# Where the next batch is scaled, turned and tidied in a state-space and feed-forward kernel

## The chip, the cores and the metric

The kernel runs on one core of one Trainium2 chip. Its time is the device time of one execution in microseconds (us); a kernel's time is the median over several executions. The engines of the core are PE (TensorE, the matrix unit, with its weight loads listed as PEld), DVE (VectorE), ACT (ScalarE), POOL (GpSimd) and SP (SyncE, here only a queue that issues transfers). Each engine takes its instructions in the order in which they stand, and waits on semaphores for the others.

## The reference

Two layers follow each other. The first is a chunked state-space layer, for 4 batches, 8 heads, 768 tokens, head size 32 and state size 16, in chunks of 32 tokens; the second is a gated feed-forward layer from 256 to 1536 and back to 256 columns.

```python
log_a = np.log(np.clip(a, 1e-06, 1.0))
state = np.zeros((batch, H, N, D), dtype=np.float32)
for c in range(nc):
    ...                                             # xc, Bc, Cc, la: this chunk
    cum = np.cumsum(la, axis=-1)
    L = np.exp(cum[:, :, :, None] - cum[:, :, None, :]) * causal
    CB = np.einsum('bhin,bhjn->bhij', Cc, Bc)
    y_intra = np.einsum('bhij,bhjd->bhid', CB * L, xc)
    y_inter = np.einsum('bhin,bhnd->bhid', Cc, state) * np.exp(cum)[:, :, :, None]
    y[:, :, sl] = y_intra + y_inter
    ...
    state = decay_full[:, :, None, None] * state + np.sum(Bx, axis=2)
x = y.transpose(0, 2, 1, 3).reshape(B * S, H * D)   # 3072 tokens x 256
out = (np.maximum(x @ w_gate, 0.0) * (x @ w_val)) @ w_out
```

Since the decay between two tokens is a product of the a between them, it can be split into a factor of the one token and the inverse factor of the other. The kernel does that: C is scaled by a running product FC, B by its reciprocal FB, and no chunk has to be treated alone.

## The kernel before

**Tiling.** The 3072 tokens are cut into 12 pairs of 128-token chunks, three pairs to a batch (`PPB`), and into 6 blocks of 512 tokens, two pairs to a block. The loop at line 442 runs over the blocks. Block b does the feed-forward layer of its 512 tokens, and in between, the state-space layer of later pairs: in the loop P = 2b+2, Q = 2b+3 and W = 2b+1.

**Preparing a batch.** Rows of B and C are loaded with `load_rows` (line 75), 384 KB each. `factors` (160) makes FC from the running product of a, with two scans and two transposes on DVE; `inverse` (179) makes FB by a reciprocal. `scale` (193) multiplies half of B or C by its factor, giving sqB and sqC: two calls for each of B and C. `turn` (202) transposes a whole sq tile on DVE into tqB or tqC. `tidy_b` (208) and `tidy_c` (220) copy a range of tq's rows, in token order, into BT and CT, where matmuls read them; CT has two halves, t = 0 and 1, masked by tmask. Eleven rows are 264 tokens, so rows 0 to 11, 11 to 22 and 22 to 32 cover the three pairs of a batch.

**A pair.** `cast_x` (231) makes bf16 xb out of the loaded xr. `rows_b` (242) transposes B back by PE (tile bb) and copies it (bt). `G` (252) multiplies B and C into four banks g; `gevac` (270) empties these with ACT (lines 277, 280) and DVE (283, 285), with POOL's causal mask (266). `astep` (290) adds a chunk to the state in the bank A_ps, and `sevac` (299) copies it, masked, to Sm on DVE; `state` (305) is both. `inter` (314) and `Dm` (326) form y from Sm and from gs, and `yevac` (340) writes yT by ACT.

**A block.** The first four of the twelve column groups f are done in two halves of 256 tokens (`gvh`, 366: tiles gv and r, product h), the others whole (`gv`, 352: tiles gate, val, r and h, ACT at 363, DVE at 364). `fout` (382) multiplies h with w_out four times, twelve matmuls each (line 387), and `foevac` (392) copies the result and stores it from SP. At the head of each block SP also issues the rows of the next batch and two pairs of x (lines 445 to 450). SP is a queue in order: these loads stand behind the preceding block's last store.

**Order.** Nothing is scheduled: `in_order` (16) fixes each engine's instructions as the Python code issues them. `prep` (456) places the preparation of batch b+1 in block b: its steps 0 and 1 at f = 4 and 5 (reciprocal, then the scales of B and C on POOL), steps 2 and 3 at f = 6 and 7 (turn B, turn C), and steps 4 to 6 at f = 8 to 10 (tidy a third of the rows of B and of C's first half on ACT, of C's second half on POOL). `at` (452) gives f for the other insertions, for blocks 0, 1, and 2 on.

**Banks.** Of the PSUM banks six are shared (`bank`, 69) by w, bb, g, gv, gate, val and o. A matmul that takes one waits for the engine that emptied it before.

**The start.** The first part of a and B go out on SP's queue, C on ACT's (lines 92 to 95). `keep_warm` (129) runs matmuls without use. The first weights are loaded by POOL (`weights`, 140) after B has landed, which `wait_for` (153) sees to.

Of the kernel before, what the change touches and what calls it, by code (L numbers as in the profile page):

```python
# [30 lines left out]
def kernel(  # L31
# [13 lines left out]
    nc = tc.nc  # L45

    NB, NH, S, D = x.shape
# [5 lines left out]
    NPAIR = T // 256  # L53
    PPB = NC // 2
    NBLK = T // 512
    R = 32
# [32 lines left out]

    al = const.tile([128, 2 * NB, K + 1], FP32)  # L90
    av = a.rearrange("b (t q) (r k) -> (q r) (b t) k", t=2, r=R)
    nc.sync.dma_start(out=al[:, 0:2, 1:], in_=av[:, 0:2])
    rows = {}
    rows["C", 0] = load_rows(C, 0, nc.scalar, "cr")
    rows["B", 0] = load_rows(B, 0, nc.sync, "br")
# [33 lines left out]
    def keep_warm(n):  # L129
        w = bank("w")  # L130
        for _ in range(n):
            nc.tensor.matmul(out=w, lhsT=warm[:, 0:128], rhs=warm, start=True, stop=True)

    keep_warm(13)

    wg = glob.tile([128, 2, DF], BF16)
    wv = glob.tile([128, 2, DF], BF16)
# [8 lines left out]
    def weights_out(f0, f1):  # L146
        nc.gpsimd.dma_start(
            out=wo[:, f0:f1, :],
            in_=moe_w_out[f0 * 128:f1 * 128, :].rearrange("(o i) m -> i o m", i=128))
# [3 lines left out]
    def wait_for(j, cell):  # L153
        nc.gpsimd.tensor_copy(gate[:, j:j + 1], cell)
# [24 lines left out]
    def inverse(b):  # L179
        nc.vector.reciprocal(FB[:, 2 * b:2 * b + 2], FC[:, 2 * b:2 * b + 2])  # L180
# [12 lines left out]
    def scale(j, b, t, eng):  # L193
        if (j, b) not in sq:
            sq[j, b] = glob.tile([128, KK, 2 * N, 2], BF16, name="sq%s%d" % (j, b))
        f = (FB if j == "B" else FC)[:, 2 * b + t].rearrange("p (a k) -> p a k", k=2)
        eng.tensor_tensor(  # L197
            out=sq[j, b][:, :, t * N:(t + 1) * N, :],
            in0=rows[j, b][:, t].rearrange("p (a k n) -> p a n k", n=N, k=2),
            in1=f.unsqueeze(2).to_broadcast([128, KK, N, 2]), op=ALU.mult)  # L200

    def turn(j, b):
        tq[j, b] = glob.tile([128, KK, R, 2], BF16, name="tq%s%d" % (j, b))
        nc.vector.transpose(  # L204
            tq[j, b].rearrange("p a r k -> p (a r k)").bitcast(U32),
            sq[j, b].rearrange("p a n k -> p (a n k)").bitcast(U32))

    def tidy_b(b, r0, r1, eng):
        dst = BT[b][:, K * r0:K * r1]
        src = tq["B", b][:, :, r0:r1, :]  # L210
        if eng is nc.scalar:
            eng.copy(out=dst.rearrange("p (r a k) -> p r a k", a=KK, k=2),
                     in_=src.rearrange("p a r k -> p r a k"))
        else:
            eng.tensor_copy(
                dst.bitcast(U32).rearrange("p (r a) -> p r a", a=KK),
                tq["B", b].rearrange("p a r k -> p (a r k)").bitcast(U32)
                .rearrange("p (a r) -> p r a", r=R)[:, r0:r1])

    def tidy_c(b, t, r0, r1, eng):  # L220
        dst = CT[b][:, t, K * r0:K * r1].rearrange("p (r a k) -> p r a k", a=KK, k=2)
        src = tq["C", b][:, :, r0:r1, :].rearrange("p a r k -> p r a k")
        if eng is nc.scalar:
            eng.mul(dst, src, tmask[:, t:t + 1])  # L224
        else:
            eng.tensor_scalar_mul(dst, src, tmask[:, t:t + 1])

    yT = glob.tile([128, 2, T], BF16)
    A_ps = mm.tile([128, 2, 128], FP32, tag="Aps", name="A_ps")
# [40 lines left out]
    def gevac(p, half=True):  # L270


        s = st[p]
        g = [t.rearrange("j i t m -> j (i t) m") for t in s["gp"]]
        d = s["gs"]
        m = maskUT.to_broadcast([128, 4, 128])
        nc.scalar.copy(out=d[:, 0], in_=g[0])  # L277
        causal(d[:, 0], 4)
        h = 2 if half else 0
        nc.scalar.copy(out=d[:, 1, h:4], in_=g[1][:, h:4])  # L280
        causal(d[:, 1, h:4], 4 - h)
        for q in (2, 3):
            nc.vector.tensor_tensor(out=d[:, q], in0=g[q], in1=m, op=ALU.mult)  # L283
        if half:
            nc.vector.tensor_tensor(out=d[:, 1, 0:2], in0=g[1][:, 0:2], in1=m[:, 0:2],
                                    op=ALU.mult)
# [18 lines left out]
    def state(p, i):  # L305
        astep(p, i)
        sevac(p, i)
# [58 lines left out]
    def gvh(b, f, u):  # L366

        if f == 0 and u == 0:
            fst[b] = ffn.tile([128, NF, 512], BF16, tag="h", name="h")
        tk = slice(b * 512 + u * 256, b * 512 + (u + 1) * 256)  # L370
        fs = slice(f * 128, (f + 1) * 128)
        gv_ = bank("gv", (128, 2, 256))
        for j, w in ((0, wg), (1, wv)):
            for k in range(2):
                nc.tensor.matmul(out=gv_[:, j], lhsT=w[:, k, fs], rhs=yT[:, k, tk],  # L375
                                 start=(k == 0), stop=(k == 1), skip_group_check=True)
        r = ffn.tile([128, 512], BF16, tag="r", name="r", bufs=3)[:, 0:256]
        nc.scalar.activation(r, gv_[:, 0], AF.Relu)  # L378
        nc.vector.tensor_tensor(out=fst[b][:, f, u * 256:(u + 1) * 256], in0=r,  # L379
                                in1=gv_[:, 1], op=ALU.mult)  # L380
# [42 lines left out]
    G(0)  # L423
    astep(0, 0)
    gevac(0, half=False)
    tidy_b(0, 11, R, nc.vector)
    sevac(0, 0)
    tidy_c(0, 0, 11, R, nc.scalar)
    tidy_c(0, 1, 11, R, nc.vector)
    wait_for(1, st[1]["xr"][0:1, 1, 0, 0:1])  # L430
    weights(4, 8)
    load_x(2, nc.sync, after=nc.gpsimd)
    keep_warm(4)
    Dm(0)
    inter(0, 1)
    astep(0, 1)
# [5 lines left out]
    for b in range(NBLK):  # L442
        P, Q, W = 2 * b + 2, 2 * b + 3, 2 * b + 1
        more = P < NPAIR
        if b < 3:
            for j, src in (("B", B), ("C", C)):
                rows[j, b + 1] = load_rows(src, b + 1, nc.sync, j.lower() + "r")
        for n in (P + 1, P + 2):
            if n < NPAIR:
                load_x(n, nc.sync)  # L450

        def at(name, *fs):

            return more and f == fs[min(b, len(fs) - 1)]

        def prep(step):
            n = b + 1
            if n >= NB:
                return
            if step == 0:  # L460
                inverse(n)
            if step < 2:
                scale("B", n, step, nc.gpsimd)
                scale("C", n, step, nc.gpsimd)
            elif step < 4:
                turn("BC"[step - 2], n)
            elif step < 7:
                r = 11 * (step - 4)
                r1 = min(r + 11, R)
                tidy_b(n, r, r1, nc.scalar)  # L470
                tidy_c(n, 0, r, r1, nc.scalar)
                tidy_c(n, 1, r, r1, nc.gpsimd)

        for f in range(4):
            gvh(b, f, 0)
            if b == 0 and f == 0:
                gevac(1)
            if b == 0 and f == 1:
                cast_x(1, nc.scalar)
                state(1, 0)  # L480
                weights(8, NF)
                wait_for(2, st[2]["xr"][0:1, 1, 0, 0:1])
                weights_out(0, NF)
            if f == (3 if b == 0 else 1):
                if b == 1:
                    state(W, 1)
                inter(W, 0)
                inter(W, 1)
                Dm(W)
                if b == 0:  # L490
                    state(1, 1)
                yevac(W, nc.scalar)
        for f in range(4):
            gvh(b, f, 1)
        for f in range(4, NF):
            if b == 0 and f == 4:
                factors(2, 8)
            gv(b, f)
            if f in (4, 5):
                prep(f - 4)  # L500
            if f >= 6:
                prep(f - 4)
            if at("cast P", 6, 4, 4):
                cast_x(P, nc.gpsimd)
            if at("cast Q", 8, 5, 4):
                cast_x(Q, nc.gpsimd)
            if at("rows P", 7, 6, 5):
                rows_b(P)
            if at("state P0", 9, 8, 7):
                state(P, 0)  # L510
            if at("state P1", 10, 10, 9):
                state(P, 1)
            if at("rows Q", 99, 9, 8):
                rows_b(Q)
        if more:
            inter(P, 0)
            inter(P, 1)
        fout(b, 0)
        foevac(b, 0)
        if more:  # L520
            G(P)
            gevac(P)
        if b == 0:
            rows_b(Q)
        fout(b, 1)
        foevac(b, 1)
        if more and b > 0:
            state(Q, 0)
        fout(b, 2)
        foevac(b, 2)  # L530
        if more:
            Dm(P)
            yevac(P, nc.scalar)
            G(Q)
            gevac(Q)
            state(Q, 1 if b else 0)
        fout(b, 3)
        foevac(b, 3)

# [31 lines left out]
```

## Time and profile before

| what | us |
|---|---|
| median of 6 runs (range) | 138.75 (138.35 to 139.23) |
| the profiled execution | 138.35 |
| its span | 136.2 |
| PE busy | 118.9 (87%) |
| DVE busy | 91.4 (67%) |
| ACT busy | 83.2 (61%) |
| POOL busy | 43.5 (32%) |
| PE clock granted | full, in all 40 slices |

The span goes from the first to the last recorded instruction; an execution takes 2.15 us more than that here. A share of busy time is an average over unlike stages, so the blocks are looked at one by one: block 0 begins at 12.76 us, blocks 1 to 5 at 37.24, 58.34, 80.39, 98.62 and 116.75. Batches 1, 2 and 3 are prepared in blocks 0, 1 and 2. In a line of the timeline the first number is the start, the second the duration; the bracket at the end gives the idle time of the engine just before and the instruction that ended it. "gs<-g" means that gs is written and g read; where several instructions are put together, xN stands behind the shapes.

### The profile page before, as it was taken

Reading aid. Unit: us, or ns where it says so; the run is one execution under the profiler, and the core shown is the slowest. Engines: PE = TensorE matmul, PEld = TensorE weight load, DVE = VectorE, ACT = ScalarE, POOL = GpSimd, SP = SyncE. Lnnn points to the kernel's source line nnn. Section 1 sums busy time; section 2 is a strip of 40 time slices with the busy share of each in tenths; the row PEclk is TensorE's granted clock in tenths of the full one; section 3 lists DMA queues with packets and bytes.
Section 4 is the critical chain, followed back from the end, with each engine's and each line's share of the span. In section 5 each row is a group of like instructions: output and inputs, shape, how many; then the busy total and the mean of one; then the engine's idle time right before and its main releaser. Section 6 shows DMA issues by size and latency. Waiting matters only on the chain.

```text
span 136.2 us, 2883 instructions
## 1 busy us (share of the span) xinstructions
PE 118.9 (87%) x1057; PEld 76.5 (56%) x1057; DVE 91.4 (67%) x204; ACT 83.2 (61%) x181; POOL 43.5 (32%) x74
## 2 busy tenths in 40 slices
PE   6957588488999967999767999999999999999990
PEld 2324463156785435786324778457785467864680
DVE  6974969576479477569377567786577865697611
ACT  4274676294587485588467478773598645886510
POOL 3435631975111981220974240102221002200000
PEclk9999999999999999999999999999999999999999
DMA  4995999950259500239800024700251002200022
GB/s 117 242 163 89 192 226 251 213 84 0 84 130 274 58 0 5 77 93 273 102 1 0 0 82 116 118 0 2 82 127 27 0 5 77 77 5 0 0 77 77
DMA packets 34686, 12.07 MB, mean 89 GB/s; under 512 B 26481, under 2 KB 34673, under 8 KB 34673
## 3 DMA queue, kind: packets, MB, share of 16 engines
q1 hardware_dynamic: 30928, 8.88, 30.4%
q0 software_dynamic: 3184, 2.36, 12.1%
q10 hardware_dynamic: 560, 0.66, 1.5%
q8 instruction: 8, 0.13, 0.4%
q14 instruction: 6, 0.04, 0.1%
HBM read 11.11 MB, written 3.15 MB: 105 GB/s over the span
## 4 chain that ended last, share of the span: by engine, by line
PE 53%; DMA 13%; ACT 8%; POOL 8%; DVE 8%; issue 6%; SPq 0%; DVEq 0%; POOLq 0%; ACTq 0%
PE o L387 20%; PE gv L375 9%; DMA br<-in_B_dram 8%; PE val L360 8%; PE gate L357 8%; DMA wv<-in_moe_w_val_dram 5%; POOL sqB L197 3%; DVE h L364 3%; PE g L259 2%; ACT r L363 2%; POOL sqC L197 2%; PE y L332 2%; ACT CT L224 2%; POOL xb L234 2%; ACT r L378 1%
## 5 line engine op out<-in xcount | busy, mean ns | idle before, releaser
L364 DVE TENSOR_TENSOR h<-r,val 128x512 bf16<-128x512 bf16 x48 | 32.5, 679 | 8.5 <-ACT r L363 8.2
L387 PE MATMUL o<-wo,h 128*128 128x256 bf16 x288 | 35.1, 273 | 2.3 <-DVE h L364 2.3
L363 ACT ACTIVATE r<-gate 128x512 bf16<-128x512 f32 x48 | 28.6, 596 | 9.8 <-PE gate L357 8.6
L387 PEld LDWEIGHTS <-h 128*128 128x128 bf16 x288 | 27.4, 98 | 7.5 <-DVE h L364 3.0
L360 PE MATMUL val<-yT,wv 128*128 128x512 bf16 x96 | 28.6, 379 | 0.9 <-DMA wv<-in_moe_w_val_dram 0.4
L357 PE MATMUL gate<-yT,wg 128*128 128x512 bf16 x96 | 28.5, 379 | 0.0
L379 DVE TENSOR_TENSOR h<-r,gv 128x256 bf16<-128x256 bf16 x48 | 20.0, 421 | 8.8 <-ACT r L378 8.3
L266 POOL TENSOR_SCALAR_AFFINE_SELECT gs<-gs 128x512 bf16<-128x512 bf16 (+1 forms) x24 | 12.1, 529 | 39.9 <-ACT gs L277 39.9
L283 DVE TENSOR_TENSOR gs<-g,maskUT 128x512 bf16<-128x512 f32 x24 | 15.5, 685 | 13.4 <-PE g L259 10.3
L378 ACT ACTIVATE r<-gv 128x256 bf16<-128x256 f32 x48 | 18.5, 385 | 4.1 <-PE gv L375 2.5
L375 PE MATMUL gv<-yT,wg 128*128 128x256 bf16 x96 | 18.4, 273 | 0.5 <-ACT yT L345 0.5
L375 PE MATMUL gv<-yT,wv 128*128 128x256 bf16 x96 | 18.3, 273 | 0.5 <-DMA wv<-in_moe_w_val_dram 0.5
L357 PEld LDWEIGHTS <-wg 128*128 128x128 bf16 x96 | 9.0, 98 | 13.5 <-issue 6.5
L360 PEld LDWEIGHTS <-wv 128*128 128x128 bf16 x96 | 9.3, 98 | 12.6 <-DMA wv<-in_moe_w_val_dram 0.9
L277 ACT CAST gs<-g 128x512 bf16<-128x512 f32 x12 | 7.0, 587 | 8.0 <-PE g L259 7.9
L345 ACT CAST yT<-y 128x512 bf16<-128x512 f32 x12 | 7.0, 585 | 7.8 <-PE y L332 6.8
L295 PE MATMUL A_ps<-xb,bt 128*128 128x256 bf16 x20 | 5.5, 274 | 6.8 <-POOL xb L234 2.9
L375 PEld LDWEIGHTS <-wg 128*128 128x128 bf16 x96 | 9.0, 98 | 4.0 <-issue 2.6
L375 PEld LDWEIGHTS <-wv 128*128 128x128 bf16 x96 | 9.3, 98 | 1.8 <-DMA wv<-in_moe_w_val_dram 0.8
L197 POOL TENSOR_TENSOR sqB<-br,FB 128x384 bf16<-128x384 f32 x6 | 5.3, 882 | 15.7 <-DVE FB L180 15.7
L224 ACT ACTIVATE CT<-tqC,tmask 128x264 bf16<-128x264 bf16 (+2 forms) x12 | 6.4, 540 | 5.2 <-DVE tqC L204 5.2
L234 POOL CAST xb<-xr 128x512 bf16<-128x512 f32 x10 | 6.1, 612 | 10.6 <-DMA xr<-in_x_dram 10.6
(65 smaller groups left out, 108.9 us busy)
## 6 DMA issues: line engine op xcount, KB each, us to landing
xr<-in_x_dram SPq DMA_DIRECT2D x24, 128.0 KB, 4.9
out_dram<-ob SPq DMA_DIRECT2D x10, 256.0 KB, 2.2
br<-in_B_dram SPq DMA_DIRECT2D x4, 384.0 KB, 4.0
cr<-in_C_dram SPq DMA_DIRECT2D x3, 384.0 KB, 4.7
wg<-in_moe_w_gate_dram POOLq DMA_DIRECT2D x3, 256.0 KB, 4.5
wv<-in_moe_w_val_dram POOLq DMA_DIRECT2D x3, 256.0 KB, 6.4
wo<-in_moe_w_out_dram POOLq DMA_DIRECT2D x1, 768.0 KB, 10.2
cr<-in_C_dram ACTq DMA_DIRECT2D x1, 384.0 KB, 3.2
```

What stands on the lines that cost most here:

```text
L197: eng.tensor_tensor(out=sq[j, b][:, :, t * N:(t + 1) * N, :], in0=rows[j, b][:, t].rearrange("p (a k n) -> p a n k", n=N, k=2), in1=f.unsq ...
L224: eng.mul(dst, src, tmask[:, t:t + 1])
L266: nc.gpsimd.affine_select(out=dst, in_=dst, pattern=[[0, n], [1, 128]], compare_op=ALU.is_ge, fill=0.0, base=0, channel_multiplier=-1)
L283: nc.vector.tensor_tensor(out=d[:, q], in0=g[q], in1=m, op=ALU.mult)
L357: nc.tensor.matmul(out=g, lhsT=wg[:, k, fs], rhs=yT[:, k, tk], start=(k == 0), stop=(k == 1))
L360: nc.tensor.matmul(out=v, lhsT=wv[:, k, fs], rhs=yT[:, k, tk], start=(k == 0), stop=(k == 1))
L363: nc.scalar.activation(r, g, AF.Relu)
L364: nc.vector.tensor_tensor(out=fst[b][:, f], in0=r, in1=v, op=ALU.mult)
L375: nc.tensor.matmul(out=gv_[:, j], lhsT=w[:, k, fs], rhs=yT[:, k, tk], start=(k == 0), stop=(k == 1), skip_group_check=True)
L378: nc.scalar.activation(r, gv_[:, 0], AF.Relu)
L379: nc.vector.tensor_tensor(out=fst[b][:, f, u * 256:(u + 1) * 256], in0=r, in1=gv_[:, 1], op=ALU.mult)
L387: nc.tensor.matmul(out=o[:, ts % 2], lhsT=fst[b][:, f, ts * 128:(ts + 1) * 128], rhs=wo[:, f], start=(f == 0), stop=(f == NF - 1), skip_gr ...
```

## The change

The first part of a is split over SP's queue and ACT's, ahead of B and of C. In the prologue only pair 1's rows are tidied, after the first state copy; the warm-up matmuls go from 13 and 4 to 14 and 3. A function `tidy(p, ...)` does one pair's rows. It stands after the first whole f of block 0 for pair 2, after its last f for pair 3, at f = 5 of later blocks for pair Q, and near the end of each block for pair P+2, on the engines given. In block 0, pair 1's first state step moves from f = 1 to f = 3, FB is made directly after the factors, and the scales follow at f = 4 to 7, C first. In later blocks the four scales are issued at f = 0 to 3 of the first quarter, and FB is made in the block before. The turns come at f = 9 and 10 of block 0, at 8 and 10 of block 1, and in block 2 after the evacuation of G(P). The cast of P's x moves from f = 6 to 5 in block 0.

```diff
-    nc.sync.dma_start(out=al[:, 0:2, 1:], in_=av[:, 0:2])
+    nc.sync.dma_start(out=al[:, 0:1, 1:], in_=av[:, 0:1])
+    nc.scalar.dma_start(out=al[:, 1:2, 1:], in_=av[:, 1:2])
...
-    keep_warm(13)
+    keep_warm(14)
...
+    def tidy(p, b_eng, c0_eng, c1_eng):
+        b, k = p // PPB, p % PPB
+        r = slice(11 * k, min(11 * k + 11, R))
+        tidy_b(b, r.start, r.stop, b_eng)
+        tidy_c(b, 0, r.start, r.stop, c0_eng)
+        tidy_c(b, 1, r.start, r.stop, c1_eng)
...
-    tidy_b(0, 11, R, nc.vector)
     sevac(0, 0)
-    tidy_c(0, 0, 11, R, nc.scalar)
-    tidy_c(0, 1, 11, R, nc.vector)
+    tidy(1, nc.vector, nc.scalar, nc.vector)
...
-    keep_warm(4)
+    keep_warm(3)
...
-        def prep(step):
-            n = b + 1
-            if n >= NB:
-                return
-            if step == 0:
-                inverse(n)
-            if step < 2:
-                scale("B", n, step, nc.gpsimd)
-                scale("C", n, step, nc.gpsimd)
-            elif step < 4:
-                turn("BC"[step - 2], n)
-            elif step < 7:
-                r = 11 * (step - 4)
-                r1 = min(r + 11, R)
-                tidy_b(n, r, r1, nc.scalar)
-                tidy_c(n, 0, r, r1, nc.scalar)
-                tidy_c(n, 1, r, r1, nc.gpsimd)
+        new = b + 1
+
+        def scale_new(k):
+            if new < NB:
+                scale("CB"[k % 2], new, k // 2, nc.gpsimd)
+
+        def turn_new(j):
+            if new < NB:
+                turn(j, new)
 
         for f in range(4):
             gvh(b, f, 0)
             if b == 0 and f == 0:
                 gevac(1)
+            if b > 0:
+                scale_new(f)
             if b == 0 and f == 1:
                 cast_x(1, nc.scalar)
-                state(1, 0)
                 weights(8, NF)
                 wait_for(2, st[2]["xr"][0:1, 1, 0, 0:1])
                 weights_out(0, NF)
+            if b == 0 and f == 3:
+                state(1, 0)
...
         for f in range(4):
             gvh(b, f, 1)
+        if b == 0:
+            factors(2, 8)
+            inverse(1)
         for f in range(4, NF):
+            gv(b, f)
             if b == 0 and f == 4:
-                factors(2, 8)
-            gv(b, f)
-            if f in (4, 5):
-                prep(f - 4)
-            if f >= 6:
-                prep(f - 4)
-            if at("cast P", 6, 4, 4):
+                tidy(P, nc.vector, nc.scalar, nc.gpsimd)
+            if b == 0 and f < 8:
+                scale_new(f - 4)
+            if at("cast P", 5, 4, 4):
                 cast_x(P, nc.gpsimd)
             if at("cast Q", 8, 5, 4):
                 cast_x(Q, nc.gpsimd)
+            if b == 0 and f == 9 or b == 1 and f == 8:
+                turn_new("C")
+            if b == 0 and f == 10 or b == 1 and f == 10:
+                turn_new("B")
+            if b == 0 and f == 11:
+                tidy(Q, nc.vector, nc.scalar, nc.gpsimd)
+            if b > 0 and more and f == 5:
+                tidy(Q, nc.scalar, nc.scalar, nc.gpsimd)
...
         if b == 0:
             rows_b(Q)
+            inverse(2)
+        if b == 1:
+            inverse(3)
+        if b == 2:
+            turn_new("C")
+            turn_new("B")
         fout(b, 1)
...
             state(Q, 1 if b else 0)
+        if P + 2 < NPAIR:
+            tidy(P + 2, nc.vector, nc.scalar, nc.gpsimd)
         fout(b, 3)
```

## The prediction

> **What bounds the kernel now.** I read the busy table by block first, cutting the span where each block's first gate matmul starts (columns: stretch and its length, then busy time of PE, PE weight load, DVE, ACT, POOL, each with its count, then clock and DMA). These are blocks 0, 1, 2 and 3:
>
> ```profile
> 12.76:37.24 24.48, 19.16 (x173) 12.23 (x174) 16.58 (x37) 14.96 (x34) 12.22 (x18) 1.00 0.89 151
> 37.24:58.34 21.10, 18.89 (x176) 12.38 (x173) 14.68 (x31) 14.17 (x32) 9.34 (x14) 1.00 0.40 88
> 58.34:80.39 22.05, 18.94 (x178) 12.59 (x176) 14.40 (x30) 14.29 (x32) 9.54 (x15) 1.00 0.38 84
> 80.39:98.62 18.23, 18.23 (x177) 12.41 (x175) 12.96 (x26) 12.13 (x26) 3.16 (x7) 1.00 0.28 60
> ```
>
> Blocks 3 and 4 are pure TensorE: 18.23 us busy in 18.23. Blocks 0 to 2, which also prepare the next batch's B and C, take 6.25, 2.87 and 3.82 us more. Only these 13 us can be won. The list of waits, kept to PE, says on what they go:
>
> ```profile
> PE A_ps L295 <- POOL xb L234: 2.9, 2, 1.9
> PE o L387 <- DVE h L364: 2.3, 3, 0.9
> PE A_ps L295 <- DVE Sm L303: 2.1, 2, 1.3
> ```
>
> PE waits for the cast of x behind POOL's scales, and for products h and states Sm that stand in DVE's queue behind the two transposes ("turn"), which wait for the scales themselves. Block 2 in the timeline (start, duration, engine, line, idle before and its releaser):
>
> ```profile
> 64.89 0.89 POOL L197 TENSOR_TENSOR sqB<-br,FB 128x384 bf16<-128x384 f32 x1 [5.95 <-DVE FB L180]
> ...
> 66.56 1.17 POOL L234 CAST xb<-xr 128x512 bf16<-128x512 f32 x2
> 67.22 0.27 PE L295 MATMUL A_ps<-xb,bt 128*128 128x256 bf16 x1 [1.00 <-POOL xb L234]
> ...
> 68.61 0.58 DVE L204 STREAM_TRANSPOSE tqB<-sqB 128x384 uint32<-128x384 uint32 x1 [2.32 <-POOL sqB L197]
> ...
> 70.61 0.27 PE L295 MATMUL A_ps<-xb,bt 128*128 128x256 bf16 x1 [1.28 <-DVE Sm L303]
> ...
> 74.75 0.28 PE L387 MATMUL o<-wo,h 128*128 128x256 bf16 x1 [0.84 <-DVE h L364]
> ```
>
> So POOL was free 5.95 us before its first scale and started it when FB came, at 64.8. But C for that batch was issued at 60.10 and took 4.7 us to land, also 64.8: an earlier scale is held by the load.
>
> **1. The split load of a.**
>
> ```profile
> 0.80 0.43 SPq L92 DMA_DIRECT2D al<-in_a_dram  x1
> 0.80 0.49 ACTq L77 DMA_DIRECT2D cr<-in_C_dram  x1
> ...
> 2.74 0.08 DVE L183 MEMSET zero<- 128x31 f32 x1
> 2.78 0.26 DVE L161 TENSOR_TENSOR_SCAN prod<-al,one 128x50 f32<-128x50 f32 x1
> ```
>
> The scan at 2.78 follows DVE's memsets without a gap, so an earlier a gains nothing. C is now issued behind a half of a: 0.49 us later, at 1.29, and no longer ahead of B. It landed at 4.0 and its scale ran at 4.46, so it lands between 4.5 and 5.3 (B's landing, if the two share evenly). That delays the first chain 0 to 0.8 us, still covered: PE began block 0's first gate matmuls at 11.94 and then stood until wv landed at 12.76 (issued 6.38, 6.4 us). The trace has a itself in 2.0 us; the Trainium skill ("DMA: Bandwidth & Descriptors", "Issuing engines are not separate DMA queues") says that loads from different queues share the same 16 DMA engines and only issue time is saved. By the row this edit is worth 0, by the rule at most 0 too, and B and wv may land later by what C no longer moves in its 0.49 us lead. Bounds 0 and +0.5; I take **+0.2**. The 14th warm-up matmul (0.43) ends before 7.4, ahead of PE's next work at 8.02.
>
> **2. Prologue order.** Sm goes ahead of the tidies, which shrink to pair 1 (DVE 0.37 for BT, about 0.4 for CT, ACT 0.53 for 0.74), one warm-up matmul less. All of it lies before the wv landing: **0**. Without that cover G of pair 1, which waited for the long CT until 11.54, would start at 11.43: a gain of 0.1.
>
> **3. Block 0, first half.** The state step of pair 1 moves from f=1 to f=3, so its Sm stands on DVE behind two more h of 0.43 us:
>
> ```profile
> 15.52 0.41 DVE L379 TENSOR_TENSOR h<-r,gv 128x256 bf16<-128x256 bf16 x1
> 15.85 0.41 DVE L303 TENSOR_TENSOR Sm<-A_ps,smask 128x256 bf16<-128x256 f32 x1
> 16.37 0.86 DVE L379 TENSOR_TENSOR h<-r,gv 128x256 bf16<-128x256 bf16 x2
> ```
>
> DVE is busy from 13.99 on, PE does the two gv's earlier but then waits for this Sm. It ends at 17.2 instead of 16.26; inter, Dm, yT and the second quarter follow: 18.46 instead of 17.63, **+0.83**.
>
> **4. Block 0, second half** is then DVE's chain. Before, from the end of the second quarter's h (20.41) to the last h (31.71) 11.30 us passed, with 1.64 us of waiting for sqB and some 1.2 for r. After: factors 1.50, reciprocal 0.45, eight h at 0.66 = 5.3, BT copy 0.35, two turns 1.14, Sm 0.41: 9.15, without a gap, since both turns now come after f=9. The BT copy of pair 2 stands behind the first h, so PE's transpose of it waits until 24.2, some 0.5 us; A_ps behind it waits for xb until 26.4 anyway. POOL isn't late: C landed at 24.06 (issued 16.16, 7.9), then scale, scale, cast end at 26.4 (27.25 before), the second pair of scales at 28.1. The last h ends at 21.24 + 9.15 = 30.39 instead of 31.71: block 0 net **-1.32**. wo lands at 28.5 (18.27 + 10.2), just ahead of fout at 28.7.
>
> **5. The tails.** In each, one tidy: DVE copy 0.37 in DVE's idle 0.42 before the next h, ACT 0.53 ahead of the output copy ob, POOL 0.95 where POOL idles. ob waited 0.31 for PE, so it slips about 0.18, and on SP the output store and the next B, C and x loads are queued behind it. Reciprocals and block 2's turns (1.14) sit behind gevac, while PE has 24 o matmuls (2.6 us) to run. PE: **0**; loads: +0.18.
>
> **6. Block 1.** C landed at 43.3 (39.0 + 4.3); now 43.3 - 1.32 + 0.18 = 42.16. On POOL all four scales now stand ahead of the cast: 4 x 0.84 + 0.6 = 3.95, so xb ends at 46.1 and A_ps starts at 46.15, where it was 46.13: PE, ready at 44.5, waits 1.65 us, and block 0's gain is eaten. Then from A_ps to the next G: before 46.13 to 53.19 = 7.06, of it turns, Sm and h waits. Now PE needs three gv (0.865 each), transpose, A_ps, y and 12 o (1.31), 4.5; DVE's second turn stands ahead of the last h and adds 0.35: 4.85. G at 51.0, i.e. 2.19 ahead: block net **-0.87**.
>
> **7. Block 2.** C at 64.8 - 2.19 + 0.18 = 62.79; cast ends 66.74, A_ps 66.8 (67.22 before) after a wait of 2.9 us. From there no turn is left in the block, and block 3 shows the undisturbed stretch, A_ps 87.90 to g 93.27 = 5.37. G at 72.17 instead of 74.97: 2.80 ahead, block net **-0.61**. Here a rule speaks against the change: the skill ("TensorE: Matmul & The Clock Gate", "HAM oscillation") warns of PE idle gaps above some 3.4 us, after which the array runs at half clock. The trace shows clock 1.00 through gaps up to 1.91 us. At 2.9 us, as worked out here, both say no loss; but 0.5 us more of waiting would by the rule cost an estimated 1.7 us (3.4 us at half speed), by the row nothing: 137.9 against 136.2. I take none, since nothing in the trace shows it, and let the range reach there.
>
> **8. Blocks 3 to 5** have tidies for pairs 9 and 11 on ACT (0.95) beside r's that leave ACT a third idle; bt would be ready 0.2 before A_ps: 0.
>
> Sum: -1.32 - 0.87 - 0.61 + 0.2 = -2.6. Span 136.2 to 133.6; the profiled run took 138.35, 2.15 around its span, giving 135.75, and the median of the runs is 0.40 above that run: **136.2 us**.
>
> **Rivals.** (a) *Block 0 gives nothing*: r or POOL leave gaps in DVE's chain, as they did before (2.9 us). For: the chain has no slack and ACT's r waits for h (three buffers). Against: the scales end (27.3 and 28.1) ahead of their turns' places in the chain (27.4 and 29.0). With 0 in place of -1.32: 137.5. (b) *The cast isn't late*: blocks 1 and 2 come down to 18.3: 5 us more, 131. For: POOL has been idle 5.9 us. Against: C's landing, read above. (c) *Slower: C lands late*. Every us of landing delay moves the cast, A_ps and block 1's end, hence also block 2's loads, and counts again there: 2 us per us. Above 1.4 us the change is slower; at 2 us late it is 140.2. For: in block 0 the same load took 7.9 us. Against: DMA there was at 0.89, in blocks 1 and 2 at 0.40. (d) *Split and prologue do more than nothing*: only if wv moves, within +-0.5.
>
> **Chances.** Forecast 0.66 (own range 135.2 to 137.2: 0.5 from the start, 0.5 per block), (a) 0.18, (b) 0.05, (c) 0.11. A measurement of this kernel tells about 0.3% (0.4 us) from no change. Faster 0.87, same 0.03, slower 0.10. Leaving out most of (b) and (c), the range is 134.6 to 138.2.
>
> **What would show it.** Sm of pair 1 near 17.2 and yT near 17.9; turns of block 0 after 27; A_ps waiting for xb about 1.7 us in block 1 and 2.9 in block 2, with scale C starting on the load's landing; G of block 3 some 2.8 us earlier; blocks 3 and 4 still 18.2. Wrong if the scales start before C's 4.3 us, if PE's clock drops in block 2, or if block 3 grows.

## The result and the profile after

The kernel with the change takes 138.74 us (median of 35 executions, 136.86 to 140.32), beside 138.44 us for the kernel before in the same measurement. The ratio is 0.9976, with a 95% interval from 0.9959 to 0.9993: 0.24% faster, within the 0.3% that this kernel's measurement can tell from no change. The forecast was 136.2 us, in a range of 134.6 to 138.2. The profiled execution of the changed kernel took 136.96 us (span 134.9, mean granted clock 0.975) and is one of its fastest: executions of one kernel differ in how many stretches of about 3.4 us TensorE spends at half clock, and a ratio leaves out those more than 1.5% above the fastest of their kernel (13 of 36 of the changed kernel), so that it is below 1 here though the median is 0.2% higher.

The busy table by block, cut at the same places as before but for block 0, whose row begins with its first gate matmul (columns as before: stretch, length, busy time of PE, weight load, DVE, ACT and POOL with counts, clock, DMA share, GB/s). Blocks 0, 1, 2 and 3 of the changed kernel:

```profile
14.37:37.22 22.85, 20.03 (x179) 12.78 (x176) 17.09 (x40) 13.68 (x31) 11.50 (x17) 0.97 0.95 162
37.22:57.43 20.21, 18.54 (x176) 12.39 (x174) 15.19 (x32) 12.87 (x30) 8.23 (x13) 1.00 0.41 92
57.43:78.69 21.26, 18.61 (x178) 12.61 (x176) 14.51 (x30) 13.35 (x30) 8.63 (x14) 1.00 0.40 87
78.69:96.92 18.23, 18.23 (x176) 12.40 (x175) 13.28 (x27) 13.09 (x29) 4.98 (x9) 1.00 0.28 60
```

Blocks 1 and 2 have become shorter by 0.89 and 0.79 us (21.10 to 20.21, 22.05 to 21.26), and block 3 is as it was. Block 0 starts later and ends at 37.22, where it ended at 37.24. Its clock of 0.97 is new. The list of waits, kept to PE, shows what each block waits for now:

```profile
PE A_ps L303 <- POOL xb L242: 4.3, 2, 2.6
PE bb L255 <- DVE BT L216: 3.5, 2, 3.1
PE y L329 <- DVE Sm L311: 1.4, 1, 1.4
```

The waits of o for h (2.3 us) and of A_ps for Sm (2.1 us) are gone. The cast xb has become the largest, 4.3 us instead of 2.9, and 3.1 us of waiting for the first BT are new. The timeline of the changed kernel's start (start, duration, engine, line, idle time before and its releaser) shows where the latter come from:

```profile
0.81 0.41 ACTq L93 DMA_DIRECT2D al<-in_a_dram  x1
1.24 0.46 ACTq L77 DMA_DIRECT2D cr<-in_C_dram  x1
...
2.75 0.23 DVE L162 TENSOR_TENSOR_SCAN prod<-al,one 128x50 f32<-128x50 f32 x1
...
6.00 1.03 DVE L198 TENSOR_TENSOR sqC<-cr,FC 128x384 bf16<-128x384 f32 x2 [1.52 <-DMA cr<-in_C_dram]
...
9.63 0.40 PE L255 MATMUL bb<-ident,BT 128*128 128x128 bf16 x2 [3.10 <-DVE BT L216]
...
14.37 0.61 PE L383 MATMUL gv<-yT,wg 128*128 128x256 bf16 x2
14.77 0.64 PE L383 MATMUL gv<-yT,wv 128*128 128x256 bf16 x2
```

The scan on a starts at 2.75 us, where it was 2.78: half a load of a is worth nothing, as forecast. But C, issued 0.44 us later than before, lands about 1.98 us later, and DVE stands 1.52 us for it. The first transpose by PE comes 1.61 us later. Then two gv matmuls take 0.61 to 0.64 us instead of 0.38: half clock, from about 8.9 to 15.7 us. The wv matmul starts 1.97 us late, and it no longer waits for wv, so the cover that the forecast relied on is used up. The same places in the timeline of the kernel before:

```profile
4.46 0.96 DVE L197 TENSOR_TENSOR sqC<-cr,FC 128x384 bf16<-128x384 f32 x2
...
8.02 0.28 PE L247 MATMUL bb<-ident,BT 128*128 128x128 bf16 x2 [1.17 <-DVE BT L215]
...
11.94 0.38 PE L375 MATMUL gv<-yT,wg 128*128 128x256 bf16 x2
...
12.80 0.39 PE L375 MATMUL gv<-yT,wv 128*128 128x256 bf16 x2 [0.48 <-DMA wv<-in_moe_w_val_dram]
```

### The profile page after: what moved, and what is told of

It is laid out like the page before. It is cut to its first block, busy times and chain, and to the rows that moved or that the text cites. A ratio compares the mean times of both kernels' runs of the same rounds, so it can differ in the third digit from the quotient of the medians.

```text
span 134.9 us, 2889 instructions
## 1 busy us (share of the span) xinstructions
PE 119.7 (89%) x1057; PEld 77.1 (57%) x1057; DVE 92.7 (69%) x210; ACT 80.8 (60%) x177; POOL 44.3 (33%) x75
## 4 chain that ended last, share of the span: by engine, by line
PE 59%; DMA 22%; POOL 6%; DVE 3%; issue 3%; ACT 3%; SPq 2%; ACTq 0%; POOLq 0%; DVEq 0%
PE o L395 23%; DMA xr<-in_x_dram 11%; PE gate L365 10%; PE val L368 10%; PE gv L383 8%; DMA wo<-in_moe_w_out_dram 8%; DMA cr<-in_C_dram 4%; PE g L267 3%; POOL sqB L198 3%; PE y L340 2%; PE A_ps L303 2%; SPq L77 1%; PE y L329 1%; POOL gs L274 1%; ACT gs L285 1%
## 5 line engine op out<-in xcount | busy, mean ns | idle before, releaser
L311 DVE TENSOR_TENSOR Sm<-A_ps,smask 128x256 bf16<-128x256 f32 x20 | 8.2, 409 | 4.0 <-PE A_ps L303 4.0
L198 POOL TENSOR_TENSOR sqC<-cr,FC 128x384 bf16<-128x384 f32 x6 | 5.3, 879 | 12.8 <-DMA cr<-in_C_dram 12.8
L225 ACT ACTIVATE CT<-tqC,tmask 128x264 bf16<-128x264 bf16 (+1 forms) x13 | 6.7, 524 | 4.4 <-DVE tqC L205 4.4
```

Of the source, the lines that this page charges most:

```text
L198: eng.tensor_tensor(out=sq[j, b][:, :, t * N:(t + 1) * N, :], in0=rows[j, b][:, t].rearrange("p (a k n) -> p a n k", n=N, k=2), in1=f.unsq ...
```

## The experiments

**Theory 1** (the mechanism): the forecast's blocks are about right; the gain is lost at the start, because the split load of a delays C by much more than its issue slot, and because PE, left idle, is then granted half clock, there and in some executions again later. **Theory 2** (rival): the moved work itself costs what was won, on DVE and POOL, and the start is a detail.

The ratios below are to the kernel before on the same chip in the same measurement (95% interval in brackets). The last column says how many stretches of 3.4 us at half clock an execution's mean clock stands for (its shortfall from 1, times twice the span, by 3.4), with the number of executions in brackets (36 for the changed kernel, one more than its median has); the kernel before has mostly one.

| kernel | median us | ratio to before | stretches at half clock |
|---|---|---|---|
| changed kernel | 138.74 | 0.9976 [0.9959, 0.9993] | 2 (17), 3 (14), 4 (5) |
| e1: a as one load | 137.33 | 0.9862 [0.9813, 0.9910] | 2 (2), 3 (4) |
| e2: kernel before, with the split only | 140.30 | 1.0098 [1.0067, 1.0129] | 1 (3), 2 (3) |
| e3: more warm-up matmuls | 138.58 | 0.9894 [0.9861, 0.9928] | 1 (10), 2 (5), 3 (7) |
| e4: both halves of a on SP | 138.63 | 0.9962 [0.9938, 0.9987] | 2 (12), 3 (6), 4 (2) |
| e5: e1, state step at f=1 | 134.97 | 0.9763 [0.9714, 0.9812] | 0 (2), 1 (2), 2 (2) |
| e6: e1, cast ahead of scales | 130.75 | 0.9471 [0.9438, 0.9504] | 1 (4), 2 (2) |
| e7: kernel before, 8 warm-ups | 138.83 | 1.0028 [1.0011, 1.0045] | 0 (13), 1 (3), 2 (5), 3 (1) |
| e8: changed kernel, cast ahead | 132.94 | 0.9637 [0.9609, 0.9665] | 2 (4), 3 (2) |
| e9: e1, state at f=1, cast ahead | 130.01 | 0.9415 [0.9393, 0.9436] | 0 (4) |
| e10: e9, with the split | 132.74 | 0.9605 [0.9569, 0.9640] | 1 (3), 2 (1), 3 (2) |
| e11: e9, cast ahead in block 0 too | 130.34 | 0.9421 [0.9398, 0.9444] | 0 (3), 1 (1) |
| e12: changed kernel, state at f=1 | 137.74 | 0.9921 [0.9889, 0.9954] | 2 (4), 4 (3) |

### The split load: e1, e2, e4 and e10

e1 undoes the split alone:

```diff
-    nc.sync.dma_start(out=al[:, 0:1, 1:], in_=av[:, 0:1])
-    nc.scalar.dma_start(out=al[:, 1:2, 1:], in_=av[:, 1:2])
+    nc.sync.dma_start(out=al[:, 0:2, 1:], in_=av[:, 0:2])
```

> The changed kernel with one part undone: the first part of a is again one load on SP's queue, and C goes first on ACT's. Theory 1 (the slot on ACT's queue): C lands at 4.0 us again instead of 6.0, its scale runs at about 4.5, PE's gap between the warm-up matmuls and the first transpose shrinks from 3.1 to about 1 us, the clock stays at 1.00, and what the rest of the change saves comes to light: block 0 some 2 us, blocks 1 and 2 some 0.8 us each, 134.9 us (134.3 to 136). Theory 2 (the moved work saves less than it costs, the split load is a side show): within 0.5 us of the changed kernel, 138 to 139 us, and the clock still below 1.

Measured: 137.33 us, ratio 0.9862, so 1.1% (1.6 us) under the changed kernel, and between the two expectations. In its profile C lands at 4.2 us, its scale runs at 4.92, and the second quarter of block 0 starts at 18.40 instead of 20.50. The start is mended; the clock is not. It is at half from 9.0 to 12.4 and from 19.2 to 22.6 us, and once more in block 2, where the timeline of e1 shows:

```profile
67.07 0.37 PE L302 MATMUL A_ps<-xb,bt 128*128 128x256 bf16 x1 [2.59 <-POOL xb L241]
67.24 1.06 PE L364 MATMUL gate<-yT,wg 128*128 128x512 bf16 x2
...
74.01 0.40 PE L266 MATMUL g<-CT,BT 32*128 32x256 bf16 x8
```

A pair of gate matmuls takes 1.06 us where it takes 0.59 at full clock, and from A_ps to G 6.94 us pass instead of the 5.30 of the changed kernel's own profile (67.96 to 73.26). So one stretch at half clock costs up to 1.64 us where PE is the limit.

e2 makes the split alone, in the kernel before: the diff above, the other way round.

> The kernel before with only the split of a over both load queues. Theory 1: C lands near 6.0 us, the first transpose of PE starts at about 9.6 instead of 8.0, PE's gap (warm-up ends at 6.5 to 6.9) is 2.8 to 3.1 us, the clock falls to half behind it for one to three stretches of about 3.4 us; start 1.6 us later less 0.8 us of cover, and half clock in a stretch where PE isn't always the limit adds 1 to 3 us: 140 to 142.5 us. Theory 2: 138.4 to 138.8 us, full clock.

Measured: 140.30 us, ratio 1.0098, slower by 1.4 us with nothing else changed, as theory 1 expected. C lands at 6.0 us, its scale runs at 6.07 (4.46 before), the first transpose at 9.70, and G after it at half clock. The second quarter starts 1.5 us late (19.14, was 17.63).

e4 keeps two loads of a, but puts both on SP's queue, so that C is first on ACT's again:

```diff
-    nc.scalar.dma_start(out=al[:, 1:2, 1:], in_=av[:, 1:2])
+    nc.sync.dma_start(out=al[:, 1:2, 1:], in_=av[:, 1:2])
```

> The changed kernel with a still in two loads, but both on SP's queue, ahead of B; C is alone and first on ACT's queue. Theory 1 (C's place on ACT's queue is what counts, not that a is cut in two): C lands near 4.0 us, B some 0.4 us later than 5.3, which the scale of B at 6.0 hides; clock 1.00 and within 0.4 us of the kernel with the whole load, 134.9 us (134.5 to 135.8). If two loads for a are themselves the harm (more transfers, a lands later): scan of a after 3.2 us and 136 us or more.

Measured: ratio 0.9962, as slow as the changed kernel; of the two expectations the second came in. C does land at 4.0 us again (3.2 us after its issue), but a's second half, issued at 1.24, takes 3.0 us, and the timeline of e4 shows the scan waiting for it:

```profile
4.33 0.26 DVE L162 TENSOR_TENSOR_SCAN prod<-al,one 128x50 f32<-128x50 f32 x1 [1.51 <-DMA al<-in_a_dram]
...
6.01 0.96 DVE L198 TENSOR_TENSOR sqC<-cr,FC 128x384 bf16<-128x384 f32 x2
```

The scan starts at 4.33, where it was 2.78 in the kernel before, and the scale of C runs at 6.01 as with the other split. So the price is not tied to one queue: with two loads of a, the scale ran at 5.7 us or later in the traces of all seven kernels that have them (4.46 to 5.17 in the seven with one load), for want of a's factor in e4 and for want of C in the others.

What happens in those first microseconds is seen in the DMA view of 0 to 4 us: queue, packets, MB, share of the 16 engines' time (q10 carries ACT's loads, q1 those of SP). The kernel before:

```profile
q10 hardware_dynamic: 272, 0.39, 31.9%
q1 hardware_dynamic: 410, 0.24, 19.4%
```

The changed kernel in the same 4 us:

```profile
q1 hardware_dynamic: 313, 0.27, 28.1%
q10 hardware_dynamic: 222, 0.13, 11.9%
```

Before, ACT's queue had moved the whole of C (0.39 MB) by 4 us, B coming behind it. With the split it has moved 0.13 MB. SP's queue gained only 0.03 MB, so it is not a mere swap of B for C: both together moved 0.40 MB instead of 0.63. The halves of a are some of the smallest loads there are here (12 KB in 128 rows of 96 bytes), and they now stand at the head of both queues. The split makes no more small packets (288 under 512 bytes in these 4 us, 289 before); why the loads behind them lose so much is not shown.

e10 puts the split into e9, the best version below, where little else is late:

> e9_all_three with the split load of a put back: the price of the split where nothing later is late. Theory 1 (C lands 1.8 to 2 us later, the cover of wv is gone, and PE's gap before the first transpose brings half clock): 1.2 to 2.2 us over e9's 130.0, so 131.2 to 132.2, with one or two half-clock stretches in the first 17 us. Theory 2 (the split costs through later blocks): within 0.4 us of e9.

Measured: 132.74 us, ratio 0.9605 against 0.9415 of e9, so 1.9% (2.6 us), more than expected. In its timeline, of an execution that took 133.38 us, the first transpose waits 3.71 us for BT (0.85 in e9), and then the clock is at half from 11 to 21 us, so that gv takes 0.63 instead of 0.38 us:

```profile
9.58 0.29 PE L255 MATMUL bb<-ident,BT 128*128 128x128 bf16 x2 [3.71 <-DVE BT L216]
...
17.21 0.63 PE L383 MATMUL gv<-yT,wg 128*128 128x256 bf16 x2
```

The split's price is thus 1.4 us (e2), 1.6 (e1), 2.3 (e8 against e6) and 2.6 us (e10 against e9). It is not a constant: in the profiles C's scale runs at 5.7 to 6.1 us in each of these kernels with the split, while the clock is at half behind it for 3.4 us in e2, 6.8 in the changed kernel and e8, and 10.2 in e10.

### The clock at the start: e3 and e7

e3 fills PE's gap ahead of the first transpose in the changed kernel:

```diff
-    keep_warm(14)
+    keep_warm(21)
```

> The changed kernel with 21 warm-up matmuls in place of 14, so that PE has work until about 9.5 us, when the first transpose's input is there; a stays split. This takes PE's gap away and leaves C's late landing. Theory 1, if the gap is what lowers the clock: clock 1.00, C at 6.0 and the first transpose at 9.6 as in the changed kernel; the late chain alone costs about 0.8 us past the cover of wv and the later weights some tenths more: 135.7 to 136.5 us, with a small spread. If the clock has another cause: clock 0.95 to 0.975 as before and 138 to 139 us.

Measured: median 138.58, where theory 1 expected 135.7 to 136.5 and a small spread (it was 136.35 to 140.03). The ratio is 0.9894 against 0.9976, a gain of 0.8%; by the medians it is 0.1%, so a gain is not certain. The profile, of an execution that took 138.74 us, shows full clock at the start (G 0.40 instead of 0.61 us) although C landed later still, at 6.4, and the transpose came at 10.14. The second quarter starts at 19.70 instead of 20.50. The clock is at half once, in block 2, behind a wait of 2.44 us for xb.

e7 does the opposite in the kernel before, by taking away five of its 13 warm-up matmuls, which is work without use:

```diff
-    keep_warm(13)
+    keep_warm(8)
```

> The kernel before with 8 warm-up matmuls at the start instead of 13; nothing else is touched, and the five are work without use. Theory 1 (an idle gap of PE brings a stretch at half clock some us later): the gap before the first transpose at 8.0 us grows from 1.2 to 3.3 us, the transposes and G after it run at half clock (one stretch of about 3.4 us more between 9 and 16 us in most executions), and what of it isn't hidden by the wait for wv at 12.8 costs 0.5 to 1.0 us: median 138.7 to 139.3, ratio 1.004 to 1.008. Theory 2 (the clock follows something other than this gap): same clock, ratio within 0.3% of 1.

Measured: ratio 1.0028, 0.4 us slower, a little less than expected, and the expected fall of the granted clock is not there: the row stays at 1.00. But the timeline of e7 shows matmuls at half speed all the same:

```profile
8.73 0.40 PE L247 MATMUL bb<-ident,BT 128*128 128x128 bf16 x2 [3.85 <-DVE BT L215]
9.06 0.62 PE L259 MATMUL g<-CT,BT 32*128 32x256 bf16 x8
```

The table of busy time by stretch for the same time in e7:

```profile
8.50:13.00 4.50, 4.27 (x40) 1.76 (x44) 3.01 (x7) 2.46 (x5) 2.63 (x5) 1.00 0.81 120
```

bb took 0.28 and G 0.40 us in the kernel before; here they take 0.40 and 0.62 beside a clock row of 1.00. So PE never had reached full speed, and the row does not show a speed that was not granted yet: the first record of the clock in this trace, at full, comes at 13.17 us (6.58 in the kernel before). That the transpose comes 0.71 us later is not the warm-ups' doing: a landed 2.7 us after its issue here (2.0 before), and the scan ran 0.70 us later. With five warm-ups too few PE runs at half clock until about 13 us, and since the kernel before waited for wv until 12.8 anyway, that costs only 0.4 us in the end. The gap ahead of the transpose matters, but cheaply as long as wv covers it. That cover is what the split used up.

### The first state step: e5 and e12

Both put the state step of pair 1 back to f = 1 of block 0, e5 with a as one load, e12 with the split:

```diff
                 cast_x(1, nc.scalar)
+                state(1, 0)
...
-            if b == 0 and f == 3:
-                state(1, 0)
```

> The changed kernel with a as one load, and the first state step of pair 1 back at f=1 of block 0. Theory 1 (what was lost lies in the start: C's landing, and half-clock stretches that follow idle gaps of PE): the later Sm cost about 0.8 us, so the second quarter starts some 0.8 us after the start that e1_whole_a had (17.6 instead of 18.4) and the wait of 1.39 us before y at 17 goes; the stretch at half clock that e1 had at 19.6 to 22.7 goes in most executions. Median 0.8 to 1.5 us under e1's 137.3. Theory 2 (the moved DVE work itself is what costs): no more than 0.3 us from e1.

> The changed kernel, split load included, with the state step of pair 1 back at f=1 alone. Theory 1 (the forecast's term of 0.83 us, and the clock on top where PE stands 1.4 us for Sm): 0.8 to 1.6 us under the changed kernel, ratio to the kernel before 0.985 to 0.992. Theory 2 (with the split, block 0 is late anyway and the order of Sm doesn't matter): within 0.3% of the changed kernel, ratio 0.996 to 1.000.

Measured, by the ratios: e5 0.9763 against 0.9862 of e1 (1.0%, 1.4 us), e12 0.9921 against 0.9976 (0.55%, 0.8 us). By the ratios e5 lies within what theory 1 expects and e12 just short of it (0.992 was the upper end); the intervals leave about 1 us either way for e5 and 0.5 for e12. The profiles give the step alone: from the first wv matmul to the second quarter of block 0 it is 5.73 us in the changed kernel and 5.07 in e12, and at full clock 5.49 in e6 (step at f = 3) and 4.82 in e5. So the step costs 0.66 to 0.67 us, where the forecast had +0.83. In e1 it comes with a stretch at half clock from 19.2 to 22.6 us, behind the 1.39 us of waiting for Sm. The profile of e5 shows neither.

### The cast: e6, e8, e9 and e11

e6 (with a as one load), e8 (with the split) and e9 (with e5's state step as well) put the cast of P's x on POOL ahead of the scales in blocks 1 and on:

```diff
+            if b > 0 and more and f == 0:
+                cast_x(P, nc.gpsimd)
             if b > 0:
                 scale_new(f)
...
-            if at("cast P", 5, 4, 4):
+            if b == 0 and f == 5:
                 cast_x(P, nc.gpsimd)
```

> The changed kernel with a as one load, and in blocks 1 and 2 the cast of P's x on POOL ahead of the four scales instead of behind them. Theory 1: PE's waits of 1.65 us (block 1) and 2.6 us (block 2) before A_ps go. Turns come at most one f later, so 3 to 4 us are won in all, and no execution shows half clock in block 2: median 132.5 to 134, clock at half in at most two stretches, all before 25 us. Theory 2 (the scales behind the cast make the turns late): A_ps starts early, but the turns then wait for sqC or sqB and PE for h, and less than 1.5 us is won: 136 or more.

> The changed kernel itself, split load of a included, with only the cast of P's x ahead of the scales in blocks 1 and 2. Theory 1: the split goes on costing what it costs between the changed kernel and e1, about 1.4 us, so this is 1 to 2 us over e6_cast_first: 134 to 135.5, and half-clock stretches only in the first 25 us. Theory 2 (the split costs only through the clock of later blocks): within 0.5 us of e6.

> a as one load, the state step of pair 1 at f=1, and the cast ahead of the scales. Theory 1: the three add up, 131.5 to 133, six to seven us under the kernel before, with C's scale still starting when C lands and the clock full from 25 us on. Theory 2: they are not independent (they share DVE in block 0, or the clock), and this is within 0.5 us of e6_cast_first.

Measured: 130.75 (ratio 0.9471), 132.94 (0.9637) and 130.01 us (0.9415). All three are better than expected, and e9 beats both kernels, by 5.9% and 5.6%. Against its counterpart without this edit, e6 is worth 3.9% (5.4 us, to e1), e8 3.4% (4.7 us, to the changed kernel) and e9 3.5% (4.8 us, to e5): the 4.3 us of waits that go, and, as it seems, the half clock that followed them (seen in e1 and e3; the table has fewer such stretches for e6 and e9). The timeline of e6 in block 1 shows the order at work:

```profile
37.89 0.62 POOL L241 CAST xb<-xr 128x512 bf16<-128x512 f32 x1
42.70 0.89 POOL L197 TENSOR_TENSOR sqC<-cr,FC 128x384 bf16<-128x384 f32 x1 [4.19 <-DMA cr<-in_C_dram]
...
45.09 0.27 PE L302 MATMUL A_ps<-xb,bt 128*128 128x256 bf16 x1
```

The cast fits into the 4.8 us in which POOL has nothing to do before C lands, and PE meets a finished xb with no wait. Theory 2 expected the turns to be late in its place; they come at 46.1 and 48.1 and nothing waits long for them. The busy table of e9 for blocks 0 to 3:

```profile
12.30:35.57 23.27, 18.96 (x172) 12.24 (x174) 17.15 (x40) 13.79 (x31) 11.49 (x17) 1.00 0.95 159
35.57:54.04 18.47, 18.39 (x174) 12.40 (x173) 14.88 (x32) 12.87 (x30) 8.23 (x13) 1.00 0.46 100
54.04:72.33 18.29, 18.24 (x176) 12.45 (x174) 14.17 (x30) 13.25 (x30) 8.48 (x13) 1.00 0.44 102
72.33:90.56 18.23, 18.18 (x175) 12.41 (x174) 13.21 (x28) 13.05 (x30) 4.97 (x9) 1.00 0.28 60
```

Blocks 1 and 2 take 18.47 and 18.29 us, as long as block 3, which prepares nothing. Only the start and block 0 are left.

e11 does the same in block 0, where PE still waits 1.38 us for this cast in e9:

```diff
             if b == 0 and f == 4:
                 tidy(P, nc.vector, nc.scalar, nc.gpsimd)
+                cast_x(P, nc.gpsimd)
...
-            if b == 0 and f == 5:
-                cast_x(P, nc.gpsimd)
```

> e9_all_three with the cast of P's x ahead of the scales in block 0 too (at f=4). PE's last long wait there is 1.38 us for this cast. If PE is the limit in block 0's second half, most of it is won: 128.6 to 129.2. If DVE's chain to the last h is (the theory of the forecast's step 4), PE only waits later for an h instead: within 0.4 us of e9's 130.0.

Measured: 130.34 us, ratio 0.9421 against 0.9415: nothing won, but for neither of the two reasons expected. The timeline of e11 shows what PE meets instead:

```profile
28.93 1.47 PE L394 MATMUL o<-wo,h 128*128 128x256 bf16 x12 [1.34 <-DMA wo<-in_moe_w_out_dram]
30.34 0.40 PE L266 MATMUL g<-CT,BT 32*128 32x256 bf16 x8
```

It waits for wo, which lands at 28.9; G starts at 30.34, and in e9 at 30.31. DVE's last h is done at 28.90 (30.04 in e9), so its chain is not the limit. The limit of block 0 has become a weight load.

## Why the prediction was wrong

The mechanisms of the blocks were right: from the second quarter of block 0 to G of block 2 they won 4.58 us, where 3.63 were forecast. The start was mis-sized by 1.84 us (20.50 instead of 18.66), and the step from the profiled execution to the median by 1.4 us more. Set beside the points of the forecast (its terms summed up to each, the 0.2 us of step 1 included; all in us):

| point | before | forecast | after |
|---|---|---|---|
| second quarter of block 0 starts | 17.63 | 18.66 | 20.50 |
| G of block 0 | 31.98 | 30.86 | 31.96 |
| G of block 1 | 53.19 | 51.2 | 52.28 |
| G of block 2 | 74.97 | 72.4 | 73.26 |
| span | 136.2 | 133.6 | 134.9 |

**Step 1 is the step that failed.** It said +0.2 with bounds 0 and +0.5, C landing between 4.5 and 5.3, "still covered" until 12.76. In its place the split cost 2.1 us at the second quarter (20.50 against 18.40 in e1, where it alone is undone) and 1.4 to 2.6 us of the whole time. C came at 6.0. The first transpose was 1.61 us late, half clock added 0.82 us between it and the first gate matmul (4.74 instead of 3.92 us), and the wait for wv gave back 0.46 us: +1.97 us at the first wv matmul. The cover was smaller than the forecast read it: from 11.94 to 12.76 PE was busy for 0.38 us with the gate matmuls, and stood only 0.48. (wv itself landed at 12.5, no later than before.) Of the 1.98 us by which C was late, 0.44 are its later issue. The forecast saw the rest half: C loses its lead and shares with B. It took B's old landing as the worst end, where the total moved in the first 4 us fell by 37%, from 0.63 to 0.40 MB. The Trainium skill's rule ("DMA: Bandwidth & Descriptors", "Issuing engines are not separate DMA queues"), that only issue time is saved by a second queue, was weighed for what could be won and for B and wv. It agrees with the trace (the scan starts 0.03 us earlier), but it says nothing of what the load behind, C, loses.

**Step 2** put the prologue at 0, on the same cover, and a gain of 0.1 without it. At full clock the new order takes 3.86 or 3.87 us from the first transpose to the first gate matmul (e5, e6, e9), and the old one 3.92: 0.05 won, so that half clock's own share of the 4.74 us is 0.87.

**Step 3** said +0.83 and Sm ending about 0.9 later. The second quarter is 2.87 us late; less the 1.97 of the start that is 0.90, of which the step itself is 0.66 (e12) and the rest half clock until 15.7 us. Near, a little too large. The timeline of the changed kernel shows it as worked out, Sm behind three h on DVE and PE waiting for it:

```profile
17.73 1.07 DVE L387 TENSOR_TENSOR h<-r,gv 128x256 bf16<-128x256 bf16 x3
18.72 0.42 DVE L311 TENSOR_TENSOR Sm<-A_ps,smask 128x256 bf16<-128x256 f32 x1
...
19.19 0.29 PE L329 MATMUL y<-CT,Sm 128*128 128x128 bf16 x2 [1.39 <-DVE Sm L311]
...
30.56 1.47 PE L395 MATMUL o<-wo,h 128*128 128x256 bf16 x12 [0.25 <-DMA wo<-in_moe_w_out_dram]
```

**Step 4** forecast 12.20 us from the start of the second quarter to G (14.35 before, less 0.83 and 1.32); 11.46 were measured. So it won 0.74 more than worked out: DVE's chain from the end of the second quarter's h to the last h took 8.33 us, not 9.15, and the last h was not waited for any more. Turning late and scaling early does what was said in block 0. Still, wo had been called just in time, and PE waits 0.25 us for it, since POOL issues it after a row of x whose arrival moved with the start.

**Steps 5 to 7.** Block 1 had to give -0.87 from G to G and gave -0.89 (21.21 to 20.32); block 2 had to give -0.61 and gave -0.80 (21.78 to 20.98). The waits for the cast were to be 1.65 and 2.9 us, with C's scale starting when C lands. POOL and PE in blocks 1 and 2 of the changed kernel:

```profile
43.62 0.89 POOL L198 TENSOR_TENSOR sqC<-cr,FC 128x384 bf16<-128x384 f32 x1 [4.95 <-DMA cr<-in_C_dram]
...
47.64 0.27 PE L303 MATMUL A_ps<-xb,bt 128*128 128x256 bf16 x1 [1.67 <-POOL xb L242]
...
63.97 0.88 POOL L198 TENSOR_TENSOR sqC<-cr,FC 128x384 bf16<-128x384 f32 x1 [5.00 <-DMA cr<-in_C_dram]
...
67.96 0.27 PE L303 MATMUL A_ps<-xb,bt 128*128 128x256 bf16 x1 [2.65 <-POOL xb L242]
```

That is as said, and the edit that removes these waits (e6, e8, e9) is worth what they measure and a little more.

**Step 7, the clock** was taken as no loss, with 137.9 us if it came. In this profile block 2 stays at full clock. In e1 and e3 it does not, after waits of 2.59 and 2.44 us, shorter than the 2.9 that the forecast held to be safe; e1 pays the 1.64 us that the rule's estimate of 1.7 had named. The Trainium skill's threshold of about 3.4 us ("TensorE: Matmul & The Clock Gate", "HAM oscillation") did not protect here; what the traces show in its place stands in the last section. Nor did the sum have a term for half clock at the start.

**Step 8** holds: blocks 3 and 4 take 18.23 and 18.12 us. From the last copy ob to the end of the span 0.41 us more pass than before (3.46 against 3.05), which no step had and no run here explains.

**From profile to median.** In the profiled execution the miss is 1.2 us (136.96 against 135.75). The other 1.4 us lie in the step to the median: the forecast added the 0.40 us of the kernel before, and the changed kernel's median is 1.78 us above its profile. The changed kernel falls to half clock more often: most executions of the kernel before show one such stretch, all of the changed kernel two to four. But their number alone does not give the time: the 17 executions with two took 136.86 to 139.06 us (median 138.31), and the profiled one is of them; those with three took 138.48 to 139.76, with four 140.00 to 140.32. That it matters where they fall is likely (in e1 one costs 1.64 us in block 2) but not shown, since only one execution of it has a trace. The split is most of the miss and not all: without it e1 comes to 136.5 us by its ratio and 137.33 by its median.

**The rivals.** (a), block 0 gives nothing, gives 137.5, and G of block 0 did stay where it was, but by another way: its second half won 2.89 us and its start lost as much. (b), the cast isn't late, 131 us, is what e6 and e9 reach by moving it (130.75 and 130.01). (c) named C's late landing, but in blocks 1 and 2, where it landed 4.6 and 4.7 us after its issue (4.3 and 4.7 were forecast); the landing that cost was that of the first C. (d) held the start within 0.5 us either way, which is wrong.

## What to carry to other kernels

Price a load that goes ahead of another by what the later one loses: not only its issue slot, but its lead over the loads that it shares the DMA engines with, and ask whether the small load was late at all (here it wasn't). On an in-order engine, work that the bounding engine waits for goes ahead of bulk work that itself waits for a transfer; that one order, a cast of 0.6 us ahead of four scales, was worth 4.7 to 5.4 us here. And a wait's price is not only its length: look at the durations of the matmuls behind it, at how much of each 3.4 us the engine worked, and at several executions, before calling it safe.

## What the runs showed of the hardware

- **Half clock follows windows with little work, not long waits as such.** In each of the fourteen traces the recorded clock changes only at points that lie 3.41 us or a multiple of it apart (in e1 at 9.00, 12.41, 19.24, 22.65, 67.03 and 70.44 us). Cut into windows of 3.41 us at such points, the first 120 us of all traces hold 457 windows at full clock. Half clock followed all eight in which PE was busy for 37% or less, three of the nine with 39 to 49%, and none of the 440 with more than 50%. What decides between 39 and 49% is open. So what counts is how much of one window a wait empties: the 2.59 us in block 2 of e1 leave PE 0.86 us of work in the window that ends at 67.03, and half clock follows; the 2.65 us in block 2 of the changed kernel fall into two windows, cut at 66.90, with 1.83 and 2.35 us of work, and it does not. At half clock, windows with 66 to 89% of work were followed by another at half clock and those with 89% or more by full clock, so that it lasted 6.8 us in the changed kernel and 10.2 in e10. The points lie elsewhere in each trace, which may be why executions of one kernel differ; that is not shown.
- **The granted-clock row and the true speed.** In the start of e7 matmuls ran at half speed with the row at 1.00. The warm-ups of the kernel before, too, took 0.43 us each (5.58 us for 13) under a row of 1.00; after them G took 0.40 us, as at full speed. The first clock record of its trace comes at 6.58 us, so "full, in all 40 slices" says nothing of the time ahead of it.
- **Small loads at the head of both queues.** The two halves of a (12 KB each) landed 1.7 to 1.8 and 1.9 to 2.0 us after issue from two queues, and 2.0 and 3.0 us after issue from one, where the whole took 2.0 to 2.7 in the seven kernels that load it so. The large loads behind them lost: in the first 4 us 0.35 to 0.45 MB moved in the six kernels with the split over two queues, 0.54 MB in e4, and 0.59 to 0.65 MB in the seven with the whole load.
